# Windowed attention and a gated MLP on one core: the transposes of q and k moved from TensorE to the DMA crossbar for batches 2 to 7

## The chip, the cores and the metric

The kernel runs on 1 core of one Trainium2 chip. The metric is device microseconds (us) of one execution; lower is better. Medians are quoted with the lowest and highest run. An experiment is always compared with runs of the kernel before on the same chip, in the same rounds. A run counts as slow when it lies over 1.5% above the fastest run of its kernel.

## The reference

There are 8 batches, 8 heads, 576 positions and 64 elements per head. Attention looks back over a window of 64 positions. Its output goes into a gated MLP whose gate mixes positions ("spatial").

```python
scores = q @ k.transpose(0, 1, 3, 2) / sqrt(64)
mask   = (rel >= 0) & (rel < 64)              # rel = query position - key position
attn   = softmax(where(mask, scores, -1e9))
x      = (attn @ v).transpose(0, 2, 1, 3).reshape(8, 576, 512)
h      = relu(x @ w_in)                       # 512 -> 1024
u, v   = h[..., :512], h[..., 512:]
v_s    = einsum('ts,bsd->btd', w_spatial, layernorm(v)) + b_spatial[None, :, None]
out    = (u * v_s) @ w_out                    # 512 -> 512
```

All inputs are f32, and q, k and v are drawn with a standard deviation of 0.1. The scores are therefore close to 0 and the softmax nearly flat, so a wrong q or k hardly changes the output. The correctness check cannot see a wrong transpose.

## The kernel before

The score product needs q and k with the 64 elements of a head on the partitions. In memory the positions come first, so q and k must be transposed. The kernel before does this on TensorE: a product with an identity matrix into the PSUM tile `tp`, then a copy by DVE (VectorE) into `qk`.

```python
def load_runs(b, x, h0, n):       # all of q, and k of batches 0 to 2: cast f32 to f16 on the way,
    nc.gpsimd.dma_start(...)      # issued by GpSimd, pieces of 1 KB (4 positions per partition)

def load_chunk(b, x, c):          # v, and k of batches 3 to 7: f32, issued by SP, pieces of 256 B
    nc.sync.dma_start(NAT[b, x][0:sn, c, :, :], ...)

def cast_pair(b, x, p):           # f32 to f16 on GpSimd
    nc.gpsimd.tensor_copy(F16[b, x][:, 0:4, hs, :], NAT[b, x][:, 0:4, hs, :])

def emit_T(b, s):                 # s = 0..3: two heads each; s = 4: the last 64 positions
    tp = psp.tile([128, 1024], f16, tag="tp", ...)
    ...
    nc.tensor.transpose(tp[...], src[:, 2 * s + h, j, :], id16[:, :])
    ...
    nc.vector.tensor_copy(qk[:, :], tp[:, 0:2 * n])
```

One batch is five attention steps. Each step takes its score products (`emit_S`, tile `sc`), exponentials on ScalarE (`emit_E`, tile `e`), sums and value products (`emit_P`, tile `oz`), and normalisation (`emit_N1`, `emit_N2`, tile `x`). The transposes of the next step and the MLP products of the two earlier batches are put between them in TensorE's program order.

```python
def att_step(i, s, nxt):
    if state["P"] is not None: emit_P(*state["P"])
    if i < B:                  emit_S(i, s)
    if state["P"] is not None: emit_N1(*state["P"])
    if nxt is not None:        emit_T(*nxt)
    if i < B:                  emit_E(i, s)
    if state["P"] is not None: emit_N2(*state["P"])
```

The stores of the output (`ob`, 4 of 256 KB and one of 128 KB per batch) also go through SP's queue. In the first batch, GpSimd casts the values of batch 0 and issues the loads of the weights, of the bias row `brow` of the spatial product and of q and k of batch 1, interleaved.

The softmax here doesn't subtract the row's maximum and nothing guards it: scores larger than these inputs give would overflow.

Of the kernel before, what the change touches and what calls it, by code (L numbers as in the profile page):

```python
# [13 lines left out]
B = 8  # L14
S = 576
BIG = 65504.0
KRUNS = 3
# [3 lines left out]
def kernel(  # L21
# [35 lines left out]

    NAT = {}
    F16 = {}
    SRC = (q, k, v)  # L60

    def new_nat(b, x):
        NAT[b, x] = inpool.tile([128, 5, 8, 64], f32, tag=f"n{'qkv'[x]}", bufs=2,
                                name=f"n{'qkv'[x]}{b}")

    def new_half(b, x):
        F16[b, x] = inpool.tile([128, 5, 8, 64], f16, tag=f"h{'qkvs'[x]}", bufs=3 if x == 0 else 2,
                                name=f"h{'qkvs'[x]}{b}")

    def in_runs(b, x):  # L70
        return x == 0 or (x == 1 and b < KRUNS)

    def runs(b, x):
        return F16[b, x][:, 0:4, :, :].rearrange("p a h d -> p (a h d)") \
            .rearrange("p (h j d) -> p h j d", h=8, j=4)

    def load_runs(b, x, h0, n):
        nc.gpsimd.dma_start(runs(b, x)[:, h0:h0 + n, :, :].rearrange("p h j d -> p h (j d)"),
                            SRC[x][b, h0:h0 + n, 0:512, :].rearrange("h (p j) d -> p h (j d)", j=4))

# [7 lines left out]
    def load_chunk(b, x, c):  # L88
        sn = 128 if c < 4 else 64
        nc.sync.dma_start(NAT[b, x][0:sn, c, :, :],  # L90
                          SRC[x][b, :, 128 * c:128 * c + sn, :].transpose([1, 0, 2]))

    def loads_soft(b):
        fs = []
        for x in (1, 0):
            if in_runs(b, x):
                fs += [lambda x=x: new_half(b, x)]
                fs += [lambda x=x, h0=h0: load_runs(b, x, h0, 4) for h0 in (0, 4)]
                fs += [lambda x=x: load_runs_rem(b, x)]
        return fs  # L100

    def loads_hard(b):
        fs = []
        for x in (1, 2):
            if not in_runs(b, x):
                fs += [lambda x=x: new_nat(b, x)]
                fs += [lambda x=x, c=c: load_chunk(b, x, c) for c in range(5)]
        return fs

    def cast_pair(b, x, p):  # L110
        hs = slice(2 * p, 2 * p + 2)
        nc.gpsimd.tensor_copy(F16[b, x][:, 0:4, hs, :], NAT[b, x][:, 0:4, hs, :])  # L112

    def shift_pair(b, p):
        hs = slice(2 * p, 2 * p + 2)
        vf, vs = NAT[b, 2], F16[b, 3]
        nc.gpsimd.tensor_copy(vs[0:64, 0:4, hs, :], vf[0:64, 0:4, hs, :])  # L117
        nc.gpsimd.tensor_copy(vs[64:128, 1:5, hs, :], vf[64:128, 0:4, hs, :])

    def cast_units(b):  # L120
        def first():
            for x in (1, 2, 3):
                if not in_runs(b, x):
                    new_half(b, x)
        steps = []
        for p in range(4):
            st = [first] if p == 0 else []
            if not in_runs(b, 1):
                st.append(lambda p=p: cast_pair(b, 1, p))
            steps.append(st + [lambda p=p: cast_pair(b, 2, p), lambda p=p: shift_pair(b, p)])  # L130
        st = []
        if not in_runs(b, 1):
            st.append(lambda: nc.gpsimd.tensor_copy(F16[b, 1][0:64, 4, :, :], NAT[b, 1][0:64, 4, :, :]))
        st.append(lambda: nc.gpsimd.tensor_copy(F16[b, 3][0:64, 4, :, :], NAT[b, 2][0:64, 4, :, :]))
        return steps + [st]
# [37 lines left out]
    for x in (1, 0):  # L173
        load_runs_rem(0, x)

# [41 lines left out]
    QK = {}  # L217
# [9 lines left out]
    def emit_T(b, s):  # L227
        tp = psp.tile([128, 1024], f16, tag="tp", bufs=1, name=f"tp{b}_{s}")
        n, off = (512, 512) if s < 4 else (256, 256)
        with nc.named_scope(f"T{b}_{s}"):  # L230
            for x in (0, 1):
                o = off if x == 1 else 0
                if s < 4 and in_runs(b, x):
                    src = runs(b, x)
                    for j in range(4):
                        for h in (0, 1):
                            nc.tensor.transpose(tp[64 * h:64 * h + 64, o + 128 * j:o + 128 * j + 128],
                                                src[:, 2 * s + h, j, :], id16[:, :])
                elif s < 4:
                    for c in range(4):  # L240
                        nc.tensor.transpose(tp[:, o + 128 * c:o + 128 * c + 128],
                                            F16[b, x][:, c, 2 * s:2 * s + 2, :], id16[:, :])
                else:
                    for p in range(4):
                        nc.tensor.transpose(tp[:, o + 64 * p:o + 64 * p + 64],  # L245
                                            F16[b, x][0:64, 4, 2 * p:2 * p + 2, :], id16[0:64, 0:64])
            qk = apool.tile([128, 2 * n], f16, tag="qk" if s < 4 else "qkr", bufs=6 if s < 4 else 2,
                            name=f"qk{b}_{s}")
            if s < 4 and in_runs(b, 1):
                nc.vector.tensor_copy(qk[:, 512:1024].rearrange("d (p j) -> d p j", j=4),  # L250
                                      tp[:, 512:1024].rearrange("d (j p) -> d p j", j=4))
                nc.vector.tensor_copy(qk[:, 0:512], tp[:, 0:512])
            else:
                nc.vector.tensor_copy(qk[:, :], tp[:, 0:2 * n])
        QK[b, s] = qk

    def emit_S(b, s):
        sc = psp.tile([128, 2, 512], f32, tag="sc", bufs=1, name=f"sc{b}_{s}")
        SC[b, s] = sc
        qk = QK[b, s]  # L260
        with nc.named_scope(f"S{b}_{s}"):
            if s < 4:
                for kap in range(8):
                    r = 64 * (kap % 2)
                    p0 = 0 if kap == 1 else 16 * kap
                    p1 = min(128, 16 * kap + 32)
                    for h in (0, 1):
                        d = slice(64 * h, 64 * h + 64)
                        nc.tensor.matmul(jp(sc[r:r + 64, h, :])[:, :, p0:p1],  # L269
                                         qk[d, 512 + 64 * kap:576 + 64 * kap],  # L270
                                         jp(qk[d, 0:512])[:, :, p0:p1],
                                         start=True, stop=True)
            else:
                for p in range(4):
                    for h in (0, 1):
                        d = slice(64 * h, 64 * h + 64)
                        nc.tensor.matmul(sc[0:64, h, 64 * p:64 * p + 64],
                                         qk[d, 256 + 64 * p:320 + 64 * p],
                                         qk[d, 64 * p:64 * p + 64], start=True, stop=True)
                    for h in (0, 1):  # L280
                        d = slice(64 * h, 64 * h + 64)
                        nc.tensor.matmul(sc[64:128, h, 64 * p:64 * p + 64],  # L282
                                         QK[b, p][d, 960:1024],
                                         qk[d, 64 * p:64 * p + 64], start=True, stop=True)
# [183 lines left out]
    def att_step(i, s, nxt):  # L468
# [6 lines left out]
        if nxt is not None:  # L475
            emit_T(*nxt)
# [19 lines left out]
    c0 = cast_units(0)  # L496
    run(c0[0])
    emit_T(0, 0)
    for s in range(5):
        if s == 0:  # L500
            load_win()
        if s < 4:
            run(c0[s + 1])
        if s == 0:
            load_wsp()
            run(loads_hard(1))
        if s == 1:
            run(loads_soft(1))
        if s == 2:
            load_wout()  # L510
        prev = state["P"]
        emit_S(0, s)
        if s < 4:
            emit_T(0, s + 1)
        warm(2)
# [3 lines left out]
        emit_E(0, s)  # L519
        if prev is not None:  # L520
            emit_N2(*prev)
# [12 lines left out]


    run(loads_hard(2))
    for st in cast_units(1):
        run(st)
    run(loads_soft(2))
# [10 lines left out]
    c2 = cast_units(2)  # L550
    l3 = loads_hard(3)
    for s in range(5):
        run(c2[s])
        run(l3, 3)
        att_step(1, s, (1, s + 1) if s < 4 else (2, 0))
        run(todo, (2, 3, 2, 2, 2)[s])
    run(todo)
    run(l3)

    for i in range(2, B + 2):  # L560
# [15 lines left out]
        soft = loads_soft(i + 1) if i + 1 < B else []  # L576
        hard = loads_hard(i + 2) if i + 2 < B else []
        casts = cast_units(i + 1) if i + 1 < B else None
        for s in range(5):
            if casts:  # L580
                run(casts[s])
            run(soft, 2)
            run(hard, 3)
            nxt = (i, s + 1) if s < 4 else (i + 1, 0)
            if nxt[0] >= B:
                nxt = None
# [33 lines left out]
```

## Time and profile before

| | kernel before |
|---|---|
| time | 236.93 us, median of 3 (235.88 to 237.28) |
| profiled span, mean granted TensorE clock | 234.5 us, 0.971 |
| one batch in the steady state | 24.33 us |

I measure a batch from its first score product to that of the next batch, as the timeline has them. These products start at 8.58, 45.76, 66.32, 88.00, 112.33, 136.66, 161.00 and 185.33 us. S(b) below means the start of batch b by this measure.

From the page of the kernel before, parts 1 and 3: busy time and share of the span of each engine with its instructions, then the DMA queues with packets, MB and share of the 16 engines' time. q1 is SP's queue, q0 the software queue that GpSimd feeds.

```profile
PE 215.6 (92%) x2745; PEld 115.9 (49%) x2745; DVE 151.8 (65%) x310; ACT 148.9 (63%) x264; POOL 113.9 (49%) x186
...
q1 hardware_dynamic: 66256, 24.78, 46.5%
q0 software_dynamic: 18896, 8.73, 29.4%
```

The windows view of the kernel before, for one batch (its neighbours are alike). The header names the columns; PEclk is the granted clock, and the DMA share can exceed 1 because the times of packets overlap.

```profile
core 0: us, PE busy (x) PEld busy (x) DVE busy (x) ACT busy (x) POOL busy (x), PEclk, DMA share, GB/s
112.33:136.66 24.33, 24.33 (x336) 13.47 (x330) 17.95 (x36) 17.92 (x32) 13.27 (x21) 1.00 0.85 172
```

TensorE is busy for the whole of the period, at the full clock, and the next engine works 18 of 24.33 us. Whatever leaves TensorE's program shortens the batch, as long as nothing else becomes the limit.

The timeline of TensorE of the kernel before, at one block of transposes: start, duration, line, operation, output and inputs.

```profile
132.87 0.41 PE L237 MATMUL tp_0_2805<-id_110,hq_2314 128*64 128x128 f16 x8
133.22 0.40 PE L241 MATMUL tp_0_2805<-id_110,hk_2307 128*128 128x128 f16 x4
133.45 0.38 PE L424 MATMUL ps_2_2828<-wspT_151,vn_0_2609 128*128 128x512 f16 x1
```

From 132.87 to the next product at 133.45 a block takes 0.58 us. Four such blocks and a remainder of 0.34 us make 2.66 us per batch. This is what the change wants to take away.

The same view of the kernel before, in the first batch; the bracket holds the idle time just before the instruction, and what ended it.

```profile
27.62 0.32 PE L320 MATMUL oz_3_518<-e_0_3_483,hv_156 128*64 128x64 f16 x4 [2.07 <-POOL hv_156 L112]
...
31.94 0.43 PE L307 MATMUL oz_4_580<-e2r_540,onesK 128*64 128x256 f16 x2 [1.59 <-DVE x_3_545 L335]
```

TensorE waits for the casts of the values of batch 0 by GpSimd. GpSimd is late because it issues loads between them. Its timeline in the kernel before has the last casts late:

```profile
16.59 0.54 POOL L210 DMA_DIRECT2D brow<-in_moe_b_spatial_dram  x1
...
26.96 0.61 POOL L112 CAST hv_156<-nv_80 128x512 f16<-128x512 f32 x1
```

### The profile page before, as it was taken

The page shows a single profiled execution, that of the slowest core. Times are in us where ns is not written, and L with a number is a line of the kernel's source. Part 1 is how long each engine was busy: PE and PEld are TensorE (multiplying, and loading weights), DVE is VectorE, ACT ScalarE, POOL GpSimd, SP SyncE. Part 2 cuts the span into 40 slices and gives each one's busy share as a digit, 9 for nine tenths or more (in the row PEclk, how much of TensorE's full clock was granted, in tenths as well). Part 3 has the DMA queues.
Part 4 walks back from the last instruction along what each step waited for, and adds up shares of the span by engine and source line. Part 5 has one row for each costly group of instructions (what it writes and reads, how often), then busy time and mean ns, then how long its engine had stood idle before and what let it go on. Part 6 is the DMA issues. An engine that isn't in the chain of part 4 may idle for free.

```text
span 234.5 us, 6590 instructions
## 1 busy us (share of the span) xinstructions
PE 215.6 (92%) x2745; PEld 115.9 (49%) x2745; DVE 151.8 (65%) x310; ACT 148.9 (63%) x264; POOL 113.9 (49%) x186
## 2 busy tenths in 40 slices
PE   7686369979899999999999999999999999999993
PEld 2353223635555465555555554565456654554450
DVE  2356226389579975877597669857785778657440
ACT  2135244835778748894689558965896589657622
POOL 7997679993269519921793169425950000000000
PEclk9889857999999999999999999999999999999999
DMA  7999999999669985999299929970930022102305
GB/s 125 230 186 209 188 182 226 185 189 210 164 165 216 184 149 106 189 246 174 28 213 238 221 21 220 239 158 4 183 105 14 3 92 67 48 1 92 113 13 188
DMA packets 85182, 33.93 MB, mean 145 GB/s; under 512 B 68064, under 2 KB 79904, under 8 KB 85152
## 3 DMA queue, kind: packets, MB, share of 16 engines
q1 hardware_dynamic: 66256, 24.78, 46.5%
q0 software_dynamic: 18896, 8.73, 29.4%
q8 instruction: 21, 0.34, 0.6%
q14 instruction: 9, 0.07, 0.1%
HBM read 32.79 MB, written 9.44 MB: 180 GB/s over the span
## 4 chain that ended last, share of the span: by engine, by line
PE 74%; DMA 8%; DVE 6%; SPq 5%; ACT 3%; issue 1%; POOL 0%; POOLq 0%
DMA nv_192<-in_v_dram 8%; SPq L90 3%; SPq L85 2%; PE pv_0_598 L360 1%; PE pv_1_609 L360 1%; PE pv_2_620 L360 1%; PE ps_0_4359 L424 1%; PE ps_0_3831 L424 1%; PE ps_0_3280 L424 1%; PE ps_0_2717 L424 1%; PE ps_0_2154 L424 1%; PE ps_1_887 L424 1%; PE ps_2_4452 L424 1%; PE ps_3_4461 L424 0%; PE ps_3_2837 L424 0%
## 5 line engine op out<-in xcount | busy, mean ns | idle before, releaser
L307 PEld LDWEIGHTS <-onesK 128*64 128x64 f16 x80 | 5.3, 107 | 15.9 <-issue 12.6
L143 PE MATMUL warm_93<-scratch 128*128 128x512 f16 x12 | 5.3, 632 | 1.3 <-DVE scratch L138 1.3
L112 POOL CAST hk_1202<-nk_751 128x512 f16<-128x512 f32 x4 | 2.8, 694 | 5.7 <-DMA nv_928<-in_v_dram 5.6
L143 PEld LDWEIGHTS <-scratch 128*128 128x128 f16 x32 | 3.0, 119 | 5.2 <-issue 3.4
L290 ACT ACTIVATE e_0_0_241<-sc_0_198 128x1024 f16<-128x1024 f32 x1 | 1.0, 1024 | 7.0 <-PE sc_0_198 L269 7.0
L404 PEld LDWEIGHTS <-win_142 128*128 128x128 f16 x32 | 3.1, 97 | 3.8
L404 PEld LDWEIGHTS <-win_143 128*128 128x128 f16 x32 | 3.1, 97 | 3.8
L404 PEld LDWEIGHTS <-win_140 128*128 128x128 f16 x32 | 3.1, 98 | 3.7 <-issue 0.4
L404 PEld LDWEIGHTS <-win_141 128*128 128x128 f16 x32 | 3.1, 98 | 3.4
L117 POOL CAST hs_1746<-nv_1417 64x512 f16<-64x512 f32 x4 | 2.9, 722 | 3.4 <-PE oz_4_1756 L320 3.4
L117 POOL CAST hs_3435<-nv_3102 64x512 f16<-64x512 f32 x4 | 2.9, 722 | 3.4 <-PE oz_4_3442 L320 3.4
L112 POOL CAST hv_2871<-nv_2539 128x512 f16<-128x512 f32 x4 | 2.4, 610 | 4.2 <-DMA nv_2539<-in_v_dram 4.2
L112 POOL CAST hk_2307<-nk_1753 128x512 f16<-128x512 f32 x4 | 2.5, 636 | 3.8 <-PE tp_4_2135 L245 3.7
L117 POOL CAST hs_2309<-nv_1976 64x512 f16<-64x512 f32 x4 | 2.9, 722 | 3.1 <-PE oz_4_2319 L320 3.1
L112 POOL CAST hk_3433<-nk_2879 128x512 f16<-128x512 f32 x4 | 2.5, 636 | 3.8 <-PE tp_4_3261 L245 3.6
L112 POOL CAST hk_2870<-nk_2316 128x512 f16<-128x512 f32 x4 | 2.5, 635 | 3.8 <-PE tp_4_2698 L245 3.7
L112 POOL CAST hv_1745<-nv_1417 128x512 f16<-128x512 f32 x4 | 2.4, 609 | 4.0 <-PE oz_3_1639 L320 4.0
L112 POOL CAST hv_2308<-nv_1976 128x512 f16<-128x512 f32 x4 | 2.4, 609 | 3.9 <-PE sc_4_2222 L282 3.9
L117 POOL CAST hs_2872<-nv_2539 64x512 f16<-64x512 f32 x4 | 2.9, 722 | 2.8 <-PE oz_4_2882 L320 2.8
L112 POOL CAST hv_3434<-nv_3102 128x512 f16<-128x512 f32 x4 | 2.4, 610 | 3.5 <-PE oz_3_3328 L320 3.5
L296 DVE TENSOR_TENSOR e2r_540<-e2r_540,maskr 128x512 f16<-128x512 f16 x1 | 0.4, 425 | 5.5 <-ACT e2r_540 L294 5.5
L117 POOL CAST hs_1204<-nv_928 64x512 f16<-64x512 f32 x4 | 2.4, 608 | 2.7 <-PE oz_4_1214 L320 2.7
(1877 smaller groups left out, 929.1 us busy)
## 6 DMA issues: line engine op xcount, KB each, us to landing
nv_80<-in_v_dram SPq DMA_DIRECT2D x9, 128.0 KB, 4.7
nv_192<-in_v_dram SPq DMA_DIRECT2D x4, 256.0 KB, 14.0
nv_551<-in_v_dram SPq DMA_DIRECT2D x4, 256.0 KB, 7.5
nk_751<-in_k_dram SPq DMA_DIRECT2D x4, 256.0 KB, 9.9
nv_928<-in_v_dram SPq DMA_DIRECT2D x4, 256.0 KB, 6.5
nk_1211<-in_k_dram SPq DMA_DIRECT2D x4, 256.0 KB, 5.7
nv_1417<-in_v_dram SPq DMA_DIRECT2D x4, 256.0 KB, 4.9
nk_1753<-in_k_dram SPq DMA_DIRECT2D x4, 256.0 KB, 5.2
```

The source lines that it names most:

```text
L85: nc.sync.dma_start(NAT[b, x][:, 0:4, h, :], SRC[x][b, h, 0:512, :].rearrange("(c p) d -> p c d", p=128))
L90: nc.sync.dma_start(NAT[b, x][0:sn, c, :, :], SRC[x][b, :, 128 * c:128 * c + sn, :].transpose([1, 0, 2]))
L112: nc.gpsimd.tensor_copy(F16[b, x][:, 0:4, hs, :], NAT[b, x][:, 0:4, hs, :])
L117: nc.gpsimd.tensor_copy(vs[0:64, 0:4, hs, :], vf[0:64, 0:4, hs, :])
L143: nc.tensor.matmul(t[:, :], scratch[:, 0:128], scratch[:, :], start=True, stop=True)
L290: nc.scalar.activation(e2[:, :, :], sc[:, :, :], AF.Exp, bias=0.0, scale=0.125)
L296: nc.vector.tensor_tensor(e2[:, :, :], e2[:, :, :], m, ALU.min)
L307: nc.tensor.matmul(oz[64 * h:64 * h + 64, 1, 0:n], onesK[:, :], e2[:, h, 0:n], start=True, stop=True)
L360: nc.tensor.matmul(pv[:, :], X[b, r][:, 128 * j:128 * j + 128], w_in_sb[r][:, 512:1024], start=(r == 0), stop=(r == 3))
L404: nc.tensor.matmul(pu[:, :], w_in_sb[r][:, 128 * m:128 * m + 128], X[b, r][:, :], start=(r == 0), stop=(r == 3))
L424: nc.tensor.matmul(ps[:, :], VN[b, kk][0:kn, 128 * m:128 * m + 128], wspT[kk][0:kn, 0:512], start=(kk == 0), stop=(kk == 4))
```

## The change

The intent has two parts. First, q and k of batches 2 to 7 are no longer transposed on TensorE. They are loaded as f32 by SP's queue and cast by GpSimd. Then `dma_start_transpose` transposes them from SBUF to SBUF through the DMA crossbar, six instructions per batch on SP's queue, straight into the layout that the score product reads. Second, the prologue is reordered: the values of batch 0 are cast before the weights are issued, and the exponentials are emitted before the sums of the step before.

```diff
-KRUNS = 3
+TB = 2
@@
     def load_runs(b, x, h0, n):
-        nc.gpsimd.dma_start(runs(b, x)[...], SRC[x][...])
+        t, eng = (F16[b, x], nc.gpsimd) if b < TB else (NAT[b, x], nc.sync)
+        eng.dma_start(runs(t)[...], SRC[x][...])
@@ (f32 tiles of q and k: one buffer each; of v: two)
-        NAT[b, x] = inpool.tile([128, 5, 8, 64], f32, tag=f"n{'qkv'[x]}", bufs=2,
+        NAT[b, x] = inpool.tile([128, 5, 8, 64], f32, tag=f"n{'qkv'[x]}", bufs=2 if x == 2 else 1,
@@
+    def tr_dma(b, x, c):
+        src = F16[b, x]
+        if c < 4:                                   # c = 0 and 2: 128 partitions x 1024
+            t = (QT, KT)[x][b]
+            nc.sync.dma_start_transpose(t[:, c:c + 2, :, :].rearrange("d c s r -> d (c s) r"),
+                                        src[:, c:c + 2, :, :].rearrange("p c h d -> p (c h d)"))
+        else:                                       # the last 64 positions: 64 x 512
+            t = (QTR, KTR)[x][b]
+            nc.sync.dma_start_transpose(t[:, :, :], src[0:64, 4, :, :].rearrange("p h d -> p (h d)"))
@@ att_step
-        if nxt is not None:
+        if nxt is not None and nxt[0] < TB:
             emit_T(*nxt)
@@ prologue, step 0
+            run(cv, 1)
             load_win()
-            run(loads_hard(1))
+            run(cv)                                 # the casts of v(0) before the other issues
             load_wsp()                              # holds the load of the bias row
+            run(loads_soft(1))
+            load_wout()
@@ prologue, every step: the exponentials ahead of the sums
+        emit_E(0, s)
         warm(2)
         if prev is not None:
             emit_P(*prev)
             emit_N1(*prev)
-        emit_E(0, s)
@@ what is put between the steps of batch i: n = i + 1, l = i + 2
+    def feed(i):
+            fs[0] += qk[0:5]                        # casts of k(n)
+            fs[1] += [..., lambda: tr_dma(n, 1, 0), lambda: tr_dma(n, 1, 2), lambda: tr_dma(n, 1, 4)] + qk[5:8]
+            fs[2] += qk[8:10] + cv[0:2]             # rest of the casts of q(n), casts of v(n)
+            fs[3] += [lambda: tr_dma(n, 0, 0), lambda: tr_dma(n, 0, 2), lambda: tr_dma(n, 0, 4)]
+            fs[2] += loads_k(l)
+            fs[3] += loads_q(l) + loads_v(l)[0:3]
+            fs[4] += loads_v(l)[3:]
... (tiles QT, KT, QTR, KTR; a gate for the loads of v(1); per-chunk casts; emit_S reads the new tiles)
```

## The prediction

> **What bounds the kernel now.** Two stages with different limits.
> (1) Steady state, 80 us to 220 us. The windows view shows stretches of 24.33 us per batch in which TensorE is busy 24.33 us, DVE 18.0, ACT 17.9, GpSimd 13.3; the chain of waits is an unbroken run of TensorE matmuls. TensorE order is the limit.
> (2) The first 33 us. TensorE is busy 6.25 us of the 13 us from 20 to 33. The timeline shows GpSimd doing value casts of batch 0 between weight-load issues, held up by the DMA ring (0.60, 0.73, 2.20, 1.14 us); TensorE's value products of block 3 and 4 of batch 0 wait for those casts: 2.07, 0.91 and 0.37 us.
>
> **What the change does.**
> - Removes the TensorE transposes of batches 2 to 7: in the timeline one block takes 0.58 us of TensorE order (132.87 to 133.45), four per batch, and the remainder 0.34: 2.66 us per batch, 16 us in all, all on the critical chain. Also removes the DVE copies out of PSUM (4 x 0.69 + 0.42 = 3.2 us per batch), off the chain.
> - Adds per batch on GpSimd five q casts (0.61 us each, +3 us), and takes away the software DMA issues (2.2 us): about 14 us of a period of 21.7. Not a limit.
> - Adds on the DMA 1.18 MB of f16 transposes per batch. The Trainium skill, "DMA: Bandwidth & Descriptors", section "Latency and other measured facts", gives 261 GB/s for a DMA transpose; from it I estimate 4.5 us per batch. No trace here shows it yet. Today the DMA works about 18.5 of each 24.3 us (one-microsecond windows: idle from 135 to 140). 18.5 + 4.5 = 23 us exceeds the 21.7 us that TensorE would then need.
> - Adds on the SP queue six transpose issues and three q loads. It now spends about 0.4 to 0.5 us per store and about 1 us per 256 KB load under load. Five stores, 13 loads and transposes of 1 to 2 us each (estimate) make 21 to 25 us per batch.
> So I expect TensorE to lose its monopoly: about 23 us per batch while loads last (batches 2 to 5), with short waits at the start of a batch for the transposed q, and 21.7 us for batches 6 and 7.
> - Prologue: casts ahead of weights and exponentials ahead of the sums free 3 to 6 us. Against it: value loads of batch 1 and loads of batch 2 now compete with the weights and may come late.
>
> **Sum.** Prologue -4.5, batch 1 -0.6, four batches -1.3 each, two batches -2.7 each, small tail effects: about -15, less 2 for new waits around 40 to 65 us: 224 us, range 214 to 239. Chances: faster 0.71, within 2% 0.19, slower 0.10.
>
> **What would show each step.** Right: no tp writes after batch 1; steady periods between 21.7 and 23.5 us; TensorE waits at the first score product of a batch ended by the DMA of the transposed q; value product of block 3 of batch 0 before 25 us without a GpSimd wait. Wrong: periods at 21.7 throughout (DMA transposes cheap, overlapped), or over 24.3 (transposes at half the assumed rate or slow to issue, SP always busy, stores late, output buffers exhausted, ACT waiting for them).
>
> **What would make it wrong.** The crossbar rate and the SP cost of a transpose are not in this trace; at 130 GB/s the DMA period would be 27 us and the kernel slower (about 242 us). Shorter distance between TensorE groups could expose ACT (17.9 of 21.7 us) through the three matmul banks. Late batch-2 loads could stall 60 to 70 us.

## The result

| | before | after |
|---|---|---|
| time | 236.76 us, median of 4 (235.88 to 237.28) | 253.31 us, median of 4 (252.67 to 255.22) |
| ratio, 95% interval | | 1.0716 (1.065 to 1.0783): slower |
| profiled span, mean granted clock | 234.5 us, 0.971 | 253.2 us, 0.926 |

Ratios are the mean time of one kernel's fast runs over that of the other's of the same rounds, so they are not quite the ratio of the medians quoted. All four runs of the changed kernel are fast. The profiled one is the longest of them, 255.22 us. So the two spans differ by 18.7 us, somewhat more than the medians (16.6 us).

The starts of the batches show where the time went. S(b) of the changed kernel is 8.27, 44.24, 70.08, 97.24, 125.00, 153.15, 181.06 and 205.74 us.

| stretch | before | after | difference | predicted |
|---|---|---|---|---|
| start to S(1) | 45.76 | 44.24 | -1.5 | -4.5 |
| S(1) to S(2) | 20.56 | 25.84 | +5.3 | -0.6 and +2 |
| S(2) to S(6), four batches with loads | 94.68 | 110.98 | +16.3 | -5.2 |
| S(6) to the end | 73.50 | 72.14 | -1.4 | -5.4 |

From the page of the changed kernel, parts 1 and 3:

```profile
PE 205.7 (81%) x2393; PEld 103.5 (41%) x2393; DVE 140.0 (55%) x278; ACT 148.5 (59%) x264; POOL 123.2 (49%) x200
...
q1 hardware_dynamic: 109248, 40.12, 76.2%
q0 software_dynamic: 7808, 4.60, 12.9%
```

TensorE lost 352 instructions, as intended, and 9.9 us of busy time. That is less than the 16 us of the prediction, since part of the remaining work ran at a lower clock (0.926 on average instead of 0.971); e2 below, at 0.970, lost 14.8 us. SP's queue grew from 66 to 109 thousand packets.

The windows view of the changed kernel; columns as before. The last line is a stretch after the last load.

```profile
97.24:125.00 27.76, 23.69 (x276) 11.68 (x276) 16.59 (x30) 17.72 (x32) 15.24 (x23) 0.93 1.08 214
125.00:153.15 28.15, 25.24 (x275) 12.06 (x275) 16.68 (x30) 17.81 (x32) 14.41 (x23) 0.89 1.06 211
...
206.00:228.00 22.00, 21.82 (x273) 11.06 (x262) 14.21 (x30) 17.55 (x32) 0.00 (x0) 1.00 0.17 55
```

These periods take 27.8 and 28.2 us, and the next one 27.91, instead of 24.33. TensorE has holes in them, and DMA is full or nearly so, with a share of 1.08, 1.06 and 0.98. One period moves 28.15 us x 211 GB/s = 5.94 MB, against 24.33 x 172 = 4.18 MB before. Of the 1.76 MB more, the transposes are 1.18 MB (two tensors of 576 x 512 in f16). The rest is q, which the profile counts at f16 size when the software queue casts it and at f32 size now. The bytes read from HBM are the same (32.79 MB on both pages). Once there are no loads, TensorE runs nearly unbroken, 21.82 of 22.00 us: the saving of the transposes is real there.

What TensorE waits for in the changed kernel, from the waits view: total us, times, longest.

```profile
PE oz_4_586 L327 <- DVE x_3_549 L355: 8.2, 1, 8.2
PE sc_0_1694 L290 <- DMA qt_1276<-hq_1283: 6.4, 1, 6.4
PE sc_0_1227 L290 <- DMA qt_815<-hq_822: 5.8, 1, 5.8
PE sc_0_3203 L290 <- DMA qt_2767<-hq_2774: 5.3, 1, 5.3
```

In five batches the first score product waits for the transposed q: three of them are shown, the other two waits are 3.6 and 2.5 us, together 23.6 us. The longest wait, 8.2 us, lies in the prologue.

Now SP's own queue in the changed kernel over most of a period, from the timeline: start, duration of the issue, line, operation, and how many instructions (their durations summed).

```profile
106.81 4.10 SPq L159 DMA_TRANSPOSE kt_1762<-hk_1676  x2
111.01 1.20 SPq L163 DMA_TRANSPOSE ktr_1764<-hk_1676  x1
...
113.53 5.18 SPq L100 DMA_DIRECT2D nk_1875<-in_k_dram  x5
118.80 0.62 SPq L467 DMA_DIRECT2D out_dram<-ob_3_1947  x1
119.52 3.30 SPq L159 DMA_TRANSPOSE qt_1761<-hq_1768  x2
122.92 1.21 SPq L163 DMA_TRANSPOSE qtr_1763<-hq_1768  x1
124.18 1.12 SPq L88 DMA_DIRECT2D nq_1983<-in_q_dram  x2
...
126.02 6.71 SPq L100 DMA_DIRECT2D nv_1987<-in_v_dram  x5
132.82 0.58 SPq L467 DMA_DIRECT2D out_dram<-ob_0_2230  x1
```

From the store of one batch's `ob_0` (at 105.67 us, ahead of this list) to that of the next at 132.82, no gap exceeds 0.2 us: SP issues from one end of the period to the other. Six transposes take 9.8 us of it, thirteen loads 13.6 us, five stores 2.7 us (two stores of 0.55 and 0.54 us and a load of 0.63 us are left out where the dots are). Over the four loaded periods the sums of the issue times are 25.5 to 27.0 us. A transpose of 64 x 512 takes 1.18 to 1.21 us to issue each time. The queue is in order, so the q transposes stand behind the loads of the next k. In the kernel before, SP issued for 13.5 us of the 24.33 from 88.00 us on (ten loads, five stores), with gaps between; two of its lines there:

```profile
91.87 3.96 SPq L90 DMA_DIRECT2D nk_1753<-in_k_dram  x3
...
99.36 2.09 SPq L90 DMA_DIRECT2D nv_1976<-in_v_dram  x2
```

The prologue of the changed kernel, timeline of TensorE:

```profile
22.47 0.41 PE L327 MATMUL oz_3_525<-e_0_3_461,onesK 128*64 128x512 f16 x2 [0.34 <-DVE x_2_492 L355]
31.87 0.42 PE L327 MATMUL oz_4_586<-e2r_518,onesK 128*64 128x256 f16 x2 [8.20 <-DVE x_3_549 L355]
```

The wait for the casts is gone: the sums and value products of block 3 now start at 22.47 us, and no wait for GpSimd is left. The next block then waits 8.20 us for `x`. The timelines of ScalarE and of GpSimd say why:

```profile
28.54 0.64 ACT L550 COPY wspT_159<-brow 1x512 f16<-1x512 f16 x1 [7.23 <-DMA brow<-in_moe_b_spatial_dram]
```

```profile
21.89 0.54 POOL L240 DMA_DIRECT2D brow<-in_moe_b_spatial_dram  x1
```

ScalarE runs in order too. It must copy the bias row before it can normalise block 3, and the bias row's load moved from 16.59 to 21.89 us, behind the casts.

### The profile page after: what moved, and what is told of

Read it like the earlier page. It is cut to its first block, busy times and chain, and to the rows that moved or that the text cites. A ratio compares the mean times of both kernels' runs of the same rounds, so it can differ in the third digit from the quotient of the medians.

```text
span 253.2 us, 5991 instructions
## 1 busy us (share of the span) xinstructions
PE 205.7 (81%) x2393; PEld 103.5 (41%) x2393; DVE 140.0 (55%) x278; ACT 148.5 (59%) x264; POOL 123.2 (49%) x200
## 3 DMA queue, kind: packets, MB, share of 16 engines
q0 software_dynamic: 7808, 4.60, 12.9%
HBM read 32.79 MB, written 9.44 MB: 167 GB/s over the span
## 4 chain that ended last, share of the span: by engine, by line
PE 31%; DMA 20%; SPq 19%; ACT 11%; DVE 6%; POOL 6%; issue 6%; POOLq 0%
SPq L100 18%; DMA nv_1057<-in_v_dram 3%; DMA nk_1381<-in_k_dram 2%; DMA nk_1875<-in_k_dram 2%; DMA hq_78<-in_q_dram 2%; DMA qt_2264<-hq_2271 2%; DMA nk_2378<-in_k_dram 2%; DMA nk_2881<-in_k_dram 2%; DMA qt_2767<-hq_2774 2%; DMA qt_1276<-hq_1283 1%; DMA qt_1761<-hq_1768 1%; DMA qt_815<-hq_822 1%; POOL hv_933 L130 1%; DMA nv_565<-in_v_dram 1%; SPq L88 1%
## 5 line engine op out<-in xcount | busy, mean ns | idle before, releaser
L148 POOL CAST hq_2774<-nq_2486 128x512 f16<-128x512 f32 x4 | 2.7, 727 | 8.3 <-DMA nq_2486<-in_q_dram 8.3
L148 POOL CAST hq_3277<-nq_2989 128x512 f16<-128x512 f32 x4 | 2.3, 612 | 7.8 <-DMA nq_2989<-in_q_dram 7.8
L148 POOL CAST hq_1768<-nq_1480 128x512 f16<-128x512 f32 x4 | 2.3, 612 | 7.5 <-DMA nq_1480<-in_q_dram 7.5
L148 POOL CAST hq_1283<-nq_1053 128x512 f16<-128x512 f32 x4 | 2.7, 725 | 6.5 <-PE pv_2_1334 L380 6.5
L290 PE MATMUL sc_0_1694<-qt_1276,kt_1277 64*64 64x128 f16 (+2 forms) x16 | 0.6, 308 | 6.4 <-DMA qt_1276<-hq_1283 6.4
L148 POOL CAST hq_2271<-nq_1983 128x512 f16<-128x512 f32 x4 | 2.3, 612 | 7.0 <-DMA nq_1983<-in_q_dram 7.0
L172 PE MATMUL warm_93<-scratch 128*128 128x512 f16 x12 | 4.4, 544 | 1.3 <-DVE scratch L167 1.3
L290 PE MATMUL sc_0_1227<-qt_815,kt_816 64*64 64x128 f16 (+2 forms) x16 | 0.6, 308 | 5.8 <-DMA qt_815<-hq_822 5.8
L424 PEld LDWEIGHTS <-win_145 128*128 128x128 f16 x32 | 3.1, 98 | 4.9 <-issue 2.0
L316 DVE TENSOR_TENSOR e_2_0_1247<-e_2_0_1247,mask 128x1024 f16<-128x1024 f16 x1 | 0.7, 693 | 8.0 <-ACT e_2_0_1247 L310 8.0
L316 DVE TENSOR_TENSOR e_3_0_1714<-e_3_0_1714,mask 128x1024 f16<-128x1024 f16 x1 | 0.7, 693 | 7.7 <-ACT e_3_0_1714 L310 7.7
L290 PE MATMUL sc_0_3203<-qt_2767,kt_2768 64*64 64x128 f16 (+2 forms) x16 | 0.6, 308 | 5.3 <-DMA qt_2767<-hq_2774 5.3
L310 ACT ACTIVATE e_3_0_1714<-sc_0_1694 128x1024 f16<-128x1024 f32 x1 | 1.0, 1024 | 6.7 <-PE sc_0_1694 L290 6.7
L310 ACT ACTIVATE e_0_0_256<-sc_0_218 128x1024 f16<-128x1024 f32 x1 | 1.0, 1024 | 6.7 <-PE sc_0_218 L290 6.7
L550 ACT COPY wspT_159<-brow 1x512 f16<-1x512 f16 x1 | 0.6, 635 | 7.2 <-DMA brow<-in_moe_b_spatial_dram 7.2
L424 PEld LDWEIGHTS <-win_146 128*128 128x128 f16 x32 | 3.1, 97 | 3.8
L424 PEld LDWEIGHTS <-win_147 128*128 128x128 f16 x32 | 3.1, 97 | 3.8
L130 POOL CAST hv_1376<-nv_1057 128x512 f16<-128x512 f32 x4 | 2.5, 615 | 4.5 <-DMA nv_1057<-in_v_dram 4.3
L130 POOL CAST hv_3379<-nv_2993 128x512 f16<-128x512 f32 x4 | 2.8, 699 | 3.7 <-PE sc_2_3404 L290 3.5
```

Of the source, the lines that this page charges most:

```text
L130: nc.gpsimd.tensor_copy(F16[b, 2][:, 0:4, hs, :], vf[:, 0:4, hs, :])
L148: nc.gpsimd.tensor_copy(o[:, c, :, :], runs(NAT[b, x])[:, :, c, :])
L172: nc.tensor.matmul(t[:, :], scratch[:, 0:128], scratch[:, :], start=True, stop=True)
L290: nc.tensor.matmul(jp(sc[r:r + 64, h, :])[:, :, p0:p1], KT[b][d, kap // 2, s, r:r + 64], QT[b][d, :, s, p0:p1], start=True, stop=True)
L310: nc.scalar.activation(e2[:, :, :], sc[:, :, :], AF.Exp, bias=0.0, scale=0.125)
L316: nc.vector.tensor_tensor(e2[:, :, :], e2[:, :, :], m, ALU.min)
```

## The experiments

Two theories stood at the start. **T**: the DMA engines' throughput is exhausted, so the bytes (or packets) of the transposes set the period. **I**: SP's issuing is exhausted, so the number of its instructions and their issue time set it. Later came O (only the order in the queue is wrong) and L (the length of a loop: load, cast, transpose, score, next load). Seventeen kernels ran. All diffs are against the changed kernel unless said otherwise. The changed kernel itself was not run again in their rounds, so a comparison with it is one between chips; the medians of the kernel before on those chips lie between 236.09 and 237.09 us. Periods are read from the one profiled execution of each kernel.

Three of them give wrong results on purpose. The check could see it in one only (e16), where parts of the output were never written; the nearly flat softmax hides wrong q and k.

### e1: the prologue alone

All batches are transposed on TensorE with the loads as before; what is left of the change is its prologue.

```diff
-TB = 2
+TB = 8
+KRUNS = 3
... (q and k loaded and transposed as in the kernel before; its order of loads)
```

> The changed kernel with all eight batches transposed on TensorE again and loaded as before; only the reordered prologue (casts ahead of weights, exponentials ahead of the sums, held-back value loads) and the new tile layout remain. If the crossbar path of batches 2 to 7 is the whole loss: score products of batch 2 at or before 66.4 us, periods of 24.3 us, time 233 to 237 us. If the reordered prologue has its own share of the loss (the score product of batch 2 came 3.7 us later in the changed kernel): 238 us or more.

Measured: 236.3 us (4 runs), before 236.09; ratio 1.0001 (0.9985 to 1.0018). The periods are 24.44 us and unbroken, and TensorE waits 8.53 us for `x` in the prologue. So the reordered prologue is worth nothing, and the crossbar with its loads is the whole loss.

### e2: no transposes

```diff
     def new_tr(b):
+        if b >= 2:
+            QT[b], KT[b], QTR[b], KTR[b] = QT[b - 2], KT[b - 2], QTR[b - 2], KTR[b - 2]
+            return
@@ tr_dma
+        return
```

> Wrong result on purpose: the changed kernel without its 36 crossbar transposes; batches 2 to 7 use the transposed tiles of batches 0 and 1. Loads, casts and TensorE work stay. If the transposes themselves are the cost (as DMA work or as issue time): periods fall from 27.9 to about 22 us and the time to 220 to 228 us. If the f32 loads of q and k on the hardware queue and the casts are the cost, periods stay over 25 us and the time over 240 us.

Measured: 225.75 us (1 run, so its state is unknown), with wrong q and k on purpose. The windows view of this kernel:

```profile
130.93:153.59 22.66, 22.22 (x280) 11.19 (x274) 16.45 (x31) 17.59 (x32) 15.06 (x23) 1.00 0.85 204
```

The saving on TensorE is real: 22.5 to 23.0 us per batch with all loads, all casts and the full clock. The 36 crossbar transposes, with the waits for what they write, cost 253.31 - 225.75 = 27.6 us. This does not say yet whether they cost it by bytes or by issuing.

### e3: half of the bytes of the large transposes

```diff
-            nc.sync.dma_start_transpose(t[:, c:c + 2, :, :]..., src[:, c:c + 2, :, :]...)
+            nc.sync.dma_start_transpose(t[:, c:c + 1, :, :]..., src[:, c:c + 1, :, :]...)
```

> Wrong result on purpose: the same 36 transposes, but the 24 large ones move half the data (one block of keys or queries instead of two). Theory T (the 16 DMA engines are saturated): about 3.4 us less DMA time per batch, periods of about 24 to 24.5 us, time 234 to 240 us. Theory I (the SP queue is full with issuing, 1.2 us or more per transpose whatever its size): no more than 2 us gained, 250 to 254 us.

Measured: 247.85 us (1 run of unknown state, wrong on purpose), periods 27.2, 26.2 and 25.75 us. It lies between the two expectations, and decides for neither.

### e4: the values loaded through GpSimd's queue

```diff
@@ load_chunk
+        eng = nc.gpsimd if x == 2 and b >= 3 else nc.sync
```

> The value loads of batches 3 to 7 are issued by GpSimd instead of SP, same bytes and same packets. Theory I: SP is freed of 6.7 to 8.6 us per batch, periods of about 22 us, time 225 to 232 us. Theory T: the DMA engines have as much to move as before; a few us at most from two queues overlapping, time 245 to 255 us.

Measured: 268.22 us (1 run of unknown state), periods near 31 us: far worse, which neither theory said. From the chain of waits of this kernel over one period (start, us, what):

```profile
133.06 3.53 PE po L464 x8
...
143.59 0.58 ACT ob L399
...
145.29 0.07 SPq L468
...
149.12 6.86 DMA nk<-in_k_dram
155.99 7.31 DMA qt<-hq
...
163.43 0.58 PE sc L291 x11
```

The period is one loop here. The score product releases the MLP products, which release a store. The store stands in SP's queue ahead of the loads of k; they land 6.9 us later, and q's transposes, behind them, 7.3 us after that. With the value loads gone from SP, SP is no longer full; it waits for `ob` tiles instead: 20.3 us between 74 and 182 us of the run, where the stores of the changed kernel wait 1.5 us. The relief was turned into a new wait. ("Same packets" in the expectation was wrong: through GpSimd's queue the values travel in packets of 4 KB, not 256 B; the page of e4 has 95 thousand packets, that of the changed kernel 117.)

### e5: four more tiny transposes per batch

```diff
@@ tr_dma, last 64 positions
+            for e in range(2):
+                nc.sync.dma_start_transpose(tiny_t[:, e:e + 1, :], src[0:16, 4, 2 * e:2 * e + 2, :]...)
```

> The changed kernel with four more crossbar transposes per batch that move almost nothing (16 partitions by 128 columns, 4 KB each, to a tile nobody reads). Theory I (every transpose holds the in-order SP queue for a fixed 1.2 us, and the DMA engines are not kept full meanwhile): 4 x 1.2 = 4.8 us more per batch in the five periods with loads, time 270 to 280 us. Theory T (the engines are the limit, SP is only held back by them): the extra issue time disappears in SP's back-pressure, time within 5 us of 253.

Measured: 286.62 and 284.49 us in the two fast runs, ratio 1.2078. A third execution took 473.59 us, and is not used; the profile fell into it, so there are no periods to read. Twenty-four transposes of 4 KB add about 32 us, 1.3 us each, though they are only 1152 packets more; in the trace, that of the slow execution, SP takes 1.22 us to issue one (median of 24). T expected next to nothing; I's 270 to 280 us was 5 us too low. So the number of transposes costs issue time on SP even where there is next to nothing to move.

### e6: two large transposes merged into one

```diff
+            if c == 2:
+                return
-            nc.sync.dma_start_transpose(t[:, c:c + 2, :, :]..., src[:, c:c + 2, :, :]...)
+            nc.sync.dma_start_transpose(t[:, :, :, :]..., src[:, 0:4, :, :]...)
```

> The two large transposes of q, and those of k, become one of twice the size: same bytes, 24 instead of 36 transposes. Theory I: two issues of about 1.25 us less per batch, periods of about 25.4 us, time 240 to 244 us. Theory T: same bytes, time within 3 us of 253.

Measured: 254.14 us (3 runs). Nothing changed. My premise was wrong: one of double size takes 2.0 to 4.3 us to issue (eleven of the twelve 2.8 us or more), where a single one takes 1.26 to 3.5 in the changed kernel. The small ones (64 x 512) take 1.18 to 1.21 there. The run tells the theories apart no better than e3.

### e7: the transposes ahead of the loads

```diff
-            fs[2] += loads_k(l)
-            fs[3] += loads_q(l) + loads_v(l)[0:3]
-            fs[4] += loads_v(l)[3:]
+            fs[3] += loads_k(l) + loads_q(l)
+            fs[4] += loads_v(l)
```

> The transposes of q of the next batch are placed ahead of the loads of k of the batch after it in the SP queue. Theory O (what hurts is only that the transposed q stands behind 1.2 MB of loads in an in-order queue): the waits of 3.6 to 6.4 us of the first score product of a batch shrink by several us each, time 230 to 242 us. Theories T and I: the queue has as much to do per batch as before, so the periods stay at 27 to 28 us, time 250 to 256 us, with at most a few us gained once at batch 2.

Measured: 252.39 us (3 runs: 250.54, 252.39 and 255.29, the last slow). S(2) comes 4.8 us earlier, at 65.31 us, so the +5.3 us of the second row of the table was the order: q(2)'s transposes stood behind the loads of k(3). But only the first loaded period is shorter (25.63 us instead of 27.16). The other three stay at 27.3 to 28.1 us, and the batch from S(6) takes 27.2 instead of 24.7 us. The gain is given back; O is refuted as the cause of the long periods.

### e8: prologue alone, with the bias row loaded early

Against e1:

```diff
+    nc.gpsimd.dma_start(brow[64:65, :], moe_b_spatial[:].unsqueeze(0))
     cv = casts_v(0)
     run(cv, 2)
@@ load_wsp
-        nc.gpsimd.dma_start(brow[64:65, :], moe_b_spatial[:].unsqueeze(0))
```

> The kernel of the first experiment (all batches on TensorE, reordered prologue) with the 1.1 KB bias row loaded ahead of the casts of batch 0. If ScalarE's in-order wait for that row (7.2 us in the changed kernel) is what ate the prologue's gain: the 8.2 us wait of TensorE before block 4 of batch 0 goes and the time falls by 4 to 7 us to 229 to 232 us. If the weights and q, k of batch 1 on the software queue bound the prologue anyway: at most 2 us gained, 234 to 237 us.

Measured: 234.1, 235.09 and 232.57 us in the fast runs, and one slow run of 238.67; ratio 0.9894 (0.9829 to 0.9959). The wait for `x` fell from 8.53 to 1.53 us, which shows that the bias row was its cause. Most of the gain is lost again at the first transpose of batch 1, as the timeline of TensorE of this kernel has it:

```profile
38.13 0.64 PE L269 MATMUL tp<-id,hq 128*64 128x128 f16 x8 [4.87 <-DMA hq<-in_q_dram]
```

So the prologue is bounded next by the loads of q and k of batch 1. About 2 us can be had there, not 4.5.

### e9: the stores issued by ScalarE

```diff
-            nc.sync.dma_start(out[o, 512:576, :], ob[64:128, :])
+            nc.scalar.dma_start(out[o, 512:576, :], ob[64:128, :])
@@ (and the four large ones likewise)
```

> The changed kernel with its 40 output stores issued by ScalarE, which has just written what they store, instead of SP: same bytes, same packets. Theory I (SP's serial issue time is the limit of the periods with loads): SP is freed of 2.7 us per batch, periods of about 25.2 us, time 238 to 243 us. Theory T (the DMA engines' throughput is the limit): the engines have as much to do, time within 4 us of 253.

Measured: 251.65 us (4 runs), ratio 1.0659 (1.0609 to 1.0708), which overlaps that of the changed kernel (1.065 to 1.0783). The windows view of this kernel:

```profile
147.24:172.29 25.05, 22.30 (x274) 11.28 (x275) 16.40 (x29) 17.09 (x31) 14.20 (x23) 1.00 1.15 235
172.29:200.13 27.84, 23.60 (x280) 11.88 (x275) 16.41 (x31) 17.51 (x32) 10.96 (x18) 0.94 0.74 169
```

The same bytes with five instructions fewer on SP: the periods S(3) to S(6) are 24.58, 25.55 and 25.05 us (the last is the first line), 25.06 on average, where the changed kernel has 27.76, 28.15 and 27.91, on average 27.94. That is 2.9 us, about what the five stores took on SP (2.7 us). No store waited for its `ob` tile in these periods of the changed kernel, so it is the stores' issue time that went. In e9 SP again issues with next to no gap: 24.5 of the 25.55 us from S(4). SP's issuing is thus the immediate limit. The total does not show it, because the time is given back elsewhere: S(2) comes 1.5 us later, the batch from S(6) takes 27.84 (second line) instead of 24.68 us, and the rest 50.1 instead of 47.5 us. And at 25.1 us the period is still longer than the 24.33 us of the kernel before.

### e10: the values loaded by ScalarE's queue

```diff
@@ load_chunk
+        eng = nc.scalar if x == 2 and b >= 3 else nc.sync
```

> The changed kernel with the value loads of batches 3 to 7 issued by ScalarE instead of SP: same hardware descriptors, same bytes. Theory I: SP is freed of 6.7 to 8.6 us per batch; what is left, about 19 to 20 us, is under the 22 us of TensorE, so periods of 22 to 24 us and 228 to 238 us, if ScalarE (17.7 us busy per batch) can take 3 to 4 us of issuing. Theory T: within 5 us of 253, or slower if ScalarE stalls in issuing.

Measured: 268.63 us (4 runs; the two fast ones 263.77 and 266.92), ratio 1.1219. The profiled execution is slow, so I read no durations from it, and whether ScalarE stalled in issuing, as T allowed, was not read. The total agrees with e4: taking the value loads off SP by another queue does not help by itself.

### e11 and e12: the crossbar for the last batch, for the last two

Both have the bias row early as in e8; batches before TB are transposed on TensorE.

```diff
-TB = 2
+TB = 7        # e11
+TB = 6        # e12
... (as e8 for the batches before TB)
```

> A candidate: the crossbar transposes for batch 7 alone, in the period where nothing is loaded any more; batches 0 to 6 on TensorE as before the change; bias row early. Against all on TensorE with the bias row early (234.6 us) TensorE saves 2.66 us and no period has both loads of a later batch and transposes: 231 to 233 us. If a transpose costs time even with idle DMA engines and SP queue: 234 us or more.

> As the candidate before it, with batches 6 and 7 on the crossbar. One period (that of batch 5) then has the loads of batch 7 and the transposes of batch 6 together. If both theories of contention hold, that period loses the 2.66 us or more that batch 6 gains: 231 to 236 us, no better than the last batch alone. If contention builds up only over several periods: 228 to 231 us.

Measured: e11 232.53 us (6 runs, two of them slow; the fast ones 231.32 to 232.65), ratio 0.9809 (0.9772 to 0.9846), faster but unclear whether by 2%. e12 **231.11 us** (229.63 to 231.28, 6 runs), ratio 0.9756 (0.9723 to 0.9789); before in the same rounds 236.62. e12 is faster than both kernels. Of its 5.5 us, about 2 are e8's, the rest is the crossbar. The windows view of e12 over the two periods in which it transposes by crossbar:

```profile
135.09:159.08 23.99, 23.90 (x324) 13.01 (x319) 17.29 (x40) 18.02 (x33) 11.13 (x17) 1.00 0.74 152
159.08:181.89 22.81, 22.23 (x276) 11.21 (x276) 16.29 (x30) 17.55 (x32) 12.19 (x18) 1.00 0.99 206
```

The period that transposes the last batch moves 22.81 x 206 = 4.70 MB, and costs nothing: it is 1.6 us shorter than the 24.44 us with transposes on TensorE.

### e13, e14, e15: combinations that should shorten the loop

e13 takes e4 and e7 together (values by GpSimd, transposes first). e14 takes e4 and e9 together (values by GpSimd, stores by ScalarE). e15 is e13 with the bias row early.

```diff
+        eng = nc.gpsimd if x == 2 and b >= 3 else nc.sync        # e13, e14, e15
+            fs[3] += loads_k(l) + loads_q(l)                     # e13, e15
+            fs[4] += loads_v(l)
+            nc.scalar.dma_start(out[o, 512:576, :], ...)         # e14, all stores
+    nc.gpsimd.dma_start(brow[64:65, :], ...)                     # e15, ahead of the first batch
```

> Values of batches 3 to 7 issued by GpSimd (as in e4) and the transposes of q ahead of the loads of k in the SP queue (as in e7). Theory L (with SP freed, what sets the period of e4 is a loop through its in-order queue: score product, product of O and its store, loads of k, transposes of q behind them, next score product): the transposes of q no longer stand behind 1.2 MB of loads, the loop is under the 22 us of TensorE, and with the issue time gone too the periods come to 22 to 24 us, time 228 to 236 us. Theory C (a second stream of loads beside SP's slows the DMA engines themselves): periods stay at 28 us or more, 255 us or more.

> Values issued by GpSimd (as in e4) and stores by ScalarE (as in e9), order of SP otherwise as in the change. Theory L: no store paces SP any more and its work per batch is about 17 us, so it runs ahead to where the tiles allow; periods of 22.5 to 25 us, time 232 to 244 us (ScalarE pays some 3 us for the stores in the chain). Theory C: periods of 28 us or more, 255 us or more.

> The kernel of e13 with the bias row loaded ahead of the casts of batch 0 (as in e8). If both mend what they are thought to mend: 2 us less than e13, 226 to 234 us. To beat e12 (231.1 us) it has to stay under that.

Measured: 254.46 us (4 runs), 262.06 us (4 runs, the two fast ones 257.81 and 261.61) and 254.12 us (6 runs). None beats the kernel before; L's numbers failed in all three. C's total held in e14 and was missed by half a microsecond in e13, but its "28 us or more" did not hold: the loaded periods are 26.7 to 28.1 us in e13, and in e14 22.53, 31.07, 25.64 and 27.23. The shortest of them moved nearly the bytes of a whole batch, after a batch that took 32.48 us:

```profile
78.55:101.08 22.53, 20.66 (x258) 10.61 (x259) 15.70 (x29) 15.74 (x29) 18.55 (x27) 0.91 1.13 258
```

So the engines moved 258 GB/s (5.80 MB) over a whole period with loads and transposes. The mix is not that of the changed kernel, though: 10633 of its packets are under 512 B, where the period of the changed kernel from 125.00 us has 14816. The chain of waits of e13 in one period shows a different loop of the same length; its longest piece:

```profile
152.25 12.89 DMA nq<-in_q_dram
```

The load of q now takes 12.9 us to land (11.4 to 13.0 in the loaded periods; 4.2 to 6.2 in the changed kernel). It stands right behind the loads of k, and those of v run beside it. Then come the casts of q and v on GpSimd, then the transposes, and only then the next loads, because the f32 tiles of q and k have one buffer. With SP relieved, the wait has moved to the landing of the loads.

### e16: half of the bytes of the stores, the same instructions

```diff
-        nc.sync.dma_start(out[b, 0:512, :]...[:, j, :], ob[:, :])
+        nc.sync.dma_start(out[b, 0:512, :]...[0:64, j, :], ob[0:64, :])
```

> The changed kernel, with the stores of the first output tiles of each batch writing only half of their partitions (wrong result on purpose): the same number of instructions on SyncE, the same order, about 0.5 MB per batch fewer bytes for the DMA engines. Theory I (the issuing of SyncE alone sets the 27.9 us period): 250 to 254 us, periods within 0.5 us of those of the changed kernel. Theory T (the throughput of the DMA engines sets it): 5.4 instead of 5.9 MB at 213 GB/s, periods 2 us or more shorter, 240 to 245 us. Both (the engines' back-pressure shows in SyncE's issuing): in between, 245 to 250 us.

Measured: 248.89 us (4 runs), ratio 1.0504 (1.0468 to 1.054); the result is wrong (unwritten rows). The windows view of this kernel:

```profile
122.68:148.91 26.23, 22.21 (x275) 11.23 (x276) 16.31 (x30) 17.70 (x32) 14.77 (x23) 1.00 1.06 205
```

With its neighbours of 27.29 and 26.80 us the average is 26.77 us, 1.2 us less than the 27.94 of the changed kernel. If throughput alone set them, 0.52 MB at 213 GB/s would have made 2.5 us; if only the count of instructions on SP did, nothing. It is half of the way. The timeline of SP shows what became shorter. The four large transposes of a batch take 5.4 to 5.9 us to issue in these three periods, where they take 6.1 to 8.5 in the changed kernel; four of the shortest would take 5.0. I read the rest as the engines' back-pressure: SP has to wait until they take more. The loads do not show this clearly: five of k take 4.8 to 5.7 us here, 5.1 to 5.3 in the changed kernel and 5.1 in e2 without any transposes; five of v take 6.5 to 6.9, 6.7 to 8.6 and, in e2, 8.8.

### e17: the crossbar for the last three batches

e12 with TB = 5. The expectation speaks of the early bias row as a gain over e12; that was a slip of mine, because e12 has it already.

> Crossbar for batches 5, 6 and 7 only, with the bias row loaded early. Compared with the kernel with the last two batches on the crossbar (231.1 us), one more period carries transposes and loads together. If a single loaded period with transposes costs what it cost in the changed kernel (27.9 against 24.3 us), this is 3 us slower than that one less the 1 to 2 us that the early bias row gives: 231 to 235 us. If the transposes harm only when several loaded periods follow one another, 228 to 231 us.

Measured: 236.62 us (4 runs), ratio 0.9981 (0.9945 to 1.0017): 5.5 us slower than e12 and outside both expectations. The windows view of this kernel:

```profile
112.96:136.87 23.91, 23.91 (x326) 12.99 (x320) 17.23 (x39) 18.03 (x32) 11.15 (x17) 1.00 0.75 153
136.87:164.22 27.35, 22.18 (x279) 11.20 (x275) 17.28 (x32) 18.00 (x33) 15.04 (x23) 0.96 1.12 215
164.22:189.17 24.95, 24.49 (x275) 11.88 (x275) 15.76 (x29) 17.34 (x31) 11.76 (x18) 0.91 0.95 190
```

The first period with transposes is free, as in e12: it moves only 23.91 x 153 = 3.66 MB, because the new order issues its loads late and carries some of them over. The second must move 27.35 x 215 = 5.88 MB, as the periods of the changed kernel do, and takes as long as they do. The third pays 2.1 us against e12, at a lower granted clock (0.91) after a wait of 4.8 us. So each full period with loads and transposes costs some 3 us, and the slow clock after its wait costs more. Another difference has nothing to do with this: the period from S(2) to S(3), without crossbar transposes, takes 26.79 us in this one profiled execution, at a clock of 0.87, against 22.64 us in e12. In its trace one DVE instruction that writes `vn` takes 2.99 us (median of the five: 0.69); TensorE waits 2.3 us for it and then runs 5.8 us at half the clock. Why that instruction was slow I did not find out. The period is 4.2 of the 7.4 us between the two spans, and S(2) came 1.8 us earlier.

## Why the prediction was wrong, point by point

**Right: TensorE bounds the steady state, and its transposes lie on the critical path.** e2 without transposes has periods of 22.5 to 23.0 us, and the changed kernel 22.00 us after its last load.

**Right: the place of the new waits.** The waits at the first score product of a batch, ended by the DMA of the transposed q, came in five batches. Only their size (2.5 to 6.4 us) was not "short".

**Wrong: "4.5 us per batch" for the transposes, and "18.5 + 4.5 = 23 us".** The figure came from the Trainium skill, "DMA: Bandwidth & Descriptors", section "Latency and other measured facts": 261 GB/s. Here are two stretches of the changed kernel, from the windows view: in the first, q's 1 KB pieces stream from HBM; in the second only transposes are under way.

```profile
126.50:128.50 2.00, 2.00 (x6) 0.66 (x5) 1.03 (x2) 1.10 (x3) 0.00 (x0) 0.50 1.06 376
201.50:204.00 2.50, 2.50 (x50) 1.47 (x47) 0.84 (x2) 2.23 (x5) 0.68 (x2) 1.00 1.09 186
```

The crossbar moves 186 GB/s while the engines' time is full. A second stretch, from 94.7 to 96.5 us, when the loads of k had landed, has 193 GB/s at a share of 1.01. In both SP issues one transpose right after the other, so the figure is what this one queue reached; that the engines could not do more is not shown. A batch's 1.18 MB thus take, by an estimate from it, 1.18 / 0.186 = 6.3 us, not 4.5. My own sum would then have been 18.5 + 6.3 = 24.8 us, over the 24.33 us of before. That q now comes in at f32 size cost the engines nothing that shows: their share times the period is 19.3 to 20.7 us in e2, which has these loads, and 18.7 to 21.2 in the kernel before. But 24.8 us is not the 27.9 us that a period took. Nor is it a firm floor: e9 moved 235 GB/s, which makes 5.94 MB / 235 = 25.3 us per batch by an estimate, and e14 had a period with 258 GB/s. That no order of the queue could win in a loaded period is therefore not shown; none of those tried won on the average of its loaded periods. The prediction named this risk ("at 130 GB/s the DMA period would be 27 us and the kernel slower (about 242 us)") and gave it too little weight.

**Wrong, the failing step: SP's queue, "21 to 25 us per batch", and the period of "about 23 us" that was read from it and from the sum above.** SP's issuing measured 25.5 to 27.0 us per batch, back to back, in periods of 27.2 to 28.2 us. The parts were nearly as I had them: the transposes within my guess of 1 to 2 us each (8.5 to 10.9 us for six), the loads 1.0 to 1.2 us each, the stores 2.7 us. But these parts add up to 21 to 27.5 us, not 21 to 25, and I took a value near the middle for the period. e9 (2.9 us less when the stores leave) and e5 (1.3 us per tiny transpose) show that SP's issuing sets the period. e16 (1.2 us less with the same instructions) shows that the engines' throughput has a part in that time.

**Wrong: batches 2 to 5 at -1.3 us each.** They took +4.1 us each (16.3 / 4), by the two steps above. A slower clock comes on top, but does not make the periods long: in that of 27.91 us TensorE is busy for only 22.22 us. The windows view of the changed kernel, just after a wait of 3.6 us and after one of 2.5 us:

```profile
125.00:131.00 6.00, 6.00 (x29) 2.40 (x30) 1.03 (x2) 2.59 (x5) 0.60 (x2) 0.50 0.95 244
...
153.20:159.00 5.80, 5.80 (x71) 2.95 (x72) 2.73 (x6) 4.83 (x8) 0.65 (x2) 1.00 1.02 248
```

At half the clock the products of 128x128 on 128x512 start every 0.43 us, where they start every 0.22 us at the full one. TensorE's busy time in these periods is 22.2 to 25.2 us for the same work, so a long wait costs up to 3 us more of TensorE's time. The Trainium skill, "TensorE: Matmul & The Clock Gate", Part 1, says that an idle window of about 3.4 us halves the clock. The waits of 3.6 and 2.5 us fit that, but other traces here do not give a limit at this length: the clock also fell after a wait of 2.07 us (kernel before, at 27.48 us) and of 2.29 us (e17), and stayed full after one of 2.59 us (e13).

**Wrong: the prologue, "free 3 to 6 us".** The step's mechanism worked (block 3 came at 22.47 us without a wait for GpSimd), but e1 shows a gain of zero. ScalarE's in-order wait for the bias row, which moved behind the casts with the weights, took all of it; e8 puts the bias row first and gains about 2 us, until the loads of batch 1 bind.

**Wrong: "21.7 us for batches 6 and 7".** The batch from S(6) took 24.68 us, of which TensorE was busy for 24.33: the wait of 5.3 us lies before S(6), and after it TensorE runs the first 6 us at a clock of 0.62. Only after the last transposes came 22.00 us.

**What stays open.** How much of SP's issue time in the 27.9 us period is the engines' back-pressure cannot be told exactly: e9 and e16 each move the period, and the two are coupled. Whether two buffers for the f32 tiles of q and k with another order would come near 25 us was not tried. What slowed one DVE instruction in the 26.79 us period of e17 is not known.

## What to carry to other kernels

Work that is taken off the bounding engine has to land somewhere with room: here DMA was at a share of 0.85, and the move added two fifths to its bytes; SP issued for 13.5 us of a period, and the move doubled that. Use the crossbar where queue and engines run dry, as for the last two batches (e12, 2.4% faster), and not in periods that are full of loads. Cost an in-order queue by the issue time of each instruction as well as by bytes, take the upper end when a rate is not in your trace, and when you move casts ahead of loads, look at which small load moves back with them and who waits for it in order.

## What the Trainium skill lacked or had wrong

- "DMA: Bandwidth & Descriptors", section "Latency and other measured facts", gives 261 GB/s for a DMA transpose, measured on one kernel with a non-contiguous middle dimension. From SBUF to SBUF, here, it was 186 and 193 GB/s in two stretches in which nothing else ran.
- "Advanced Engine Details and Errata", section "X-Bar Transpose (TRN2)", says that transposes are as fast as regular DMAs and expects 350 to 400 GB/s. Here it was 186 GB/s. A packet of a transpose took 23.2 ns of an engine's time (1880 packets in 2.5 us at a share of 1.092, over 16 engines), a packet of a plain load of 256 B pieces in the kernel before 17.7 ns (1222 packets in 1.4 us at a share of 0.965, 219 GB/s). Plain pieces of 1 KB streamed at 376 GB/s.
- No page that I read gives, for trn2 by name, the time that SP needs to issue a transpose. Here it was 1.2 us at the least even for 4 KB (1.22 us, in a slow execution), at least 1.26 us for 128 x 1024 (changed kernel) and 2.0 us for twice that (e6). Landing took 2.4 us for 64 x 512, and 3.3 to 5.6 us for the large ones.
- "DMA: Bandwidth & Descriptors", section "Issuing engines are not separate DMA queues", says that another issuing engine saves only the issue time, "usually small relative to the DMA itself". That all share the same engines fits e13, where q took 11.4 to 13.0 us to land with the values on another queue. The issue time was not small here: 2.9 us of a 27.9 us period for five stores (e9).
- "TensorE: Matmul & The Clock Gate", Part 1, names an idle window of about 3.4 us. The traces agree that the clock goes to 0.50 after a long wait (3.6 us), but it also did after 2.07 and 2.29 us, and not after 2.55 and 2.59 us.
